# An attention and state-space kernel on one core: overdue SSM steps get a turn on VectorE, SSM units wait for their buffers before a bank, PV takes any ready tile, and 18 slots

## The chip, the cores and the metric

The kernel runs on one core of a Trainium2 chip. The metric is the device time of one execution, in microseconds (us). Engines are named as the profile names them: PE is TensorE (matmuls), PEld its weight loads, DVE is VectorE, ACT is ScalarE, POOL is GpSimd, SP is SyncE. "Span" is the time from the first to the last instruction of the profiled execution, some 1.7 us less than the time of that execution.

## The reference

Two independent halves are computed from their own inputs and joined along the last axis, to 1 x 2048 x 1280 in bf16. Cut to what matters:

```python
def ssm(x, ...):                      # 2048 steps, 640 states, complex
    Bu = einsum("bld,pd->blp", x, B_bar)
    for t in range(L):
        h = Lam_bar * h + Bu[t]       # diagonal: a scan for each state
    return 2 * einsum(h, C).real + x * Dskip

def attention(x, wq, wk, wv, wo):     # 32 query heads of 20, one key/value head
    scores = einsum("bhqd,bkd->bhqk", q, k) * 20 ** -0.5
    return einsum("bhqk,bkd->bhqd", softmax(scores), v) @ wo
```

The attention has 32 x 2048 x 2048 scores, and each wants an exponential. That is the large piece of work. The kernel cuts it into 2048 tiles of 128 keys x 512 query rows: 32 blocks of 64 tiles.

## The kernel before

A Python program orders the instructions when the kernel is built. It keeps a list of operations, each with an engine, an estimated duration, dependences and a priority (lower goes first), plays them against a clock of its own, and writes one fixed stream for each engine with semaphores between them. So a change of a priority changes no arithmetic; it changes the order of the streams, and which engine a tile falls to. The choice on each engine:

```python
    def pick(self, eng):
        ...                                   # `can`: all operations that could start now
        for op in can:
            p, dur = op.prio, op.dur
            if eng == "pe" and op.mode != self.mode:
                dur += self.SWITCH
                if p > self.URGENT:
                    p += self.STAY
            if urgent is not None and p > self.URGENT and t + dur > urgent + self.slack.get(eng, 1e9):
                continue
            if best is None or (p, op.seq) < key:
                best, key = op, (p, op.seq)
        return best
```

The exponential of a tile is taken on one of two engines. ScalarE empties score banks in turns of three and of two tiles (`PR<-SC`, 1536 and 1024 columns; with scores held in banks called SC). VectorE takes single tiles, called D tiles here: one eviction (`DR<-MB`) writes an integer whose bits are roughly the exponential, and three scaled copies of it (`DR<-DR`, for one tile or for two at once) correct the shape of the curve; four matmuls then use them. A D tile is taken when a side bank (MB) and four buffers ("slots") are free:

```python
    NDS = 16                                  # slots
    SHARE = 0.25

    def want_d(self, taken=0):
        s = self.s
        if self.tile_n >= NTILE - 8 or self.d_count + taken + 1 > self.SHARE * (self.tile_n - 16):
            return False
        if len(self.d_banks()) <= taken:
            return False
        return len(self.d_free()) > taken + len(self.SHIFTS) - 1
```

The share of tiles on VectorE is thus no constant; it falls out of how soon VectorE frees banks and slots. The product with the values (PV) keeps a queue for each of the four row groups, and looks at the head of each queue:

```python
        for j in range(4):                    # in pv_source
            if q[j]:
                e = q[j][0]
                if e[4].end is not None and s.seen(e[4], "pe") <= t and self.vp_seen(e[1], t):
                    group.append((j, e))
```

The state-space half (SSM) runs beside the attention as background: 40 half units (a projection on TensorE in one of two side banks, then on VectorE products, a scan and products again) and 20 output pieces ("y pieces"), dated evenly over the tiles. The side banks also carry the D tiles. On VectorE the SSM steps have priority 3, against 0.5 for the D tiles' steps, so they run when there is nothing else to do. `unit_ready` asks only for the data of a unit, and a unit can take a bank while the buffer into which its product goes is still in use:

```python
    def gate_of(self, key):
        o = self.buf_user.get(key)
        return lambda: o is None or o.start is not None

    SSM_FROM, SSM_TO = 110, 1830
        ...                                   # in background
        step = (self.SSM_TO - self.SSM_FROM) / len(jobs)
        ...
            T.append((self.SSM_FROM + step * i, 2) + job)

    def unit_ready(self, tb, c, ri):
        if ri == 1:
            return (tb, c, 0) in self.p_op
        ...                                   # tables, inputs, the unit before
```

## Time and profile before

| | before |
|---|---|
| median of the runs | 796.67 us (796.21 to 798.23, 4 runs) |
| profiled run, its span | 796.33 us, 794.6 us |
| mean granted clock | 1.000 |
| ScalarE busy / VectorE busy / TensorE busy | 772.1 / 730.9 / 732.6 us |
| tiles on ScalarE / on VectorE | 1668 / 380 |

From the page of before: busy time of each engine, VectorE's busy share in tenths for 40 equal slices of the span, the chain of work that ended last, and the costliest groups (out<-in, count, busy us and mean ns of one, idle time of the engine just before them and what ended most of it).

```profile
PE 732.6 (92%) x10441; PEld 240.5 (30%) x10441; DVE 730.9 (92%) x1818; ACT 772.1 (97%) x692; POOL 13.5 (2%) x35
...
DVE  6999999999999989999999999898999996789794
...
ACT 82%; PE 10%; DVE 5%; DMA 1%; issue 1%; ACTq 0%; DVEq 0%
...
L1007 ACT ACTIVATE PR<-SC 128x1536 bf16<-128x1536 f32 (+1 forms) x667 | 755.3, 1452 | 5.2 <-PE SC L538 3.2
...
L553 DVE TENSOR_SCALAR DR<-MB 128x512 int16<-128x512 f32 x380 | 254.2, 682 | 25.2 <-PE MB L538 23.3
...
L553 DVE TENSOR_SCALAR DR<-DR 128x512 int16<-128x512 int16 (+1 forms) x890 | 241.5, 320 | 6.6 <-PE MB L538 3.3
```

ScalarE is busy for 97% of the span and its exponentials are 82% of the chain. The other two engines show 92%, but they are not the bound: TensorE waits 37.8 us for ScalarE's banks (by the page, before its score matmuls) and VectorE 23.3 us for scores. VectorE's row of tenths is the second thing to see. It has room in it near the end (6, 7, 8, 9, 7, 9), where the steps of the SSM units are over (the last one on VectorE starts at 654.7 us).

The same groups by form, and a stretch of ScalarE's timeline (start, length, instructions; in brackets the idle time before and what ended it):

```profile
L1007 ACT ACTIVATE PR<-SC 128x1536 bf16<-128x1536 f32 x334 | 555.5, 1663 | 3.9 <-PE SC L538 2.9 <-PE MB L538 0.9
L1007 ACT ACTIVATE PR<-SC 128x1024 bf16<-128x1024 f32 x333 | 413.2, 1241 | 1.3 <-PE MB L538 0.8 <-PE SC L538 0.3
```

```profile
25.06 5.97 ACT L1007 ACTIVATE PR<-SC 128x1536 bf16<-128x1536 f32 x5 [2.08 <-PE SC L538]
...
105.09 95.03 ACT L1007 ACTIVATE PR<-SC 128x1024 bf16<-128x1024 f32 x84
...
754.52 28.89 ACT L1007 ACTIVATE PR<-SC 128x1536 bf16<-128x1536 f32 x25
```

The sum of the two forms, 968.7 us, is longer than the span, because neighbouring exponentials overlap. The pitch is the honest cost: 84 of them, 42 of each form, in 95.03 us are 2.262 us for five tiles, 0.4525 us a tile. The Trainium skill, "ScalarE: Activation LUTs", section "What ACT_TABLE_LOAD costs", gives 0.833 ns for an element of a row and an overlap of about 93 ns between neighbours. The trace agrees on the first, (1663 - 1241) / 512 = 0.82 ns; the overlap is longer by these records, 1663 + 1241 - 2262 = 642 ns for two, so 321 ns each.

25.06 us pass until the first exponential (the head), and 11.2 us from the end of the last one, 783.41, to the end (the tail).

ScalarE's waits (line waiting, what for, us in total, times, longest), and a table of stretches (stretch, length, then busy us and count of PE, PEld, DVE, ACT and POOL, granted clock, DMA share, GB/s):

```profile
ACT PR L1007 <- PE SC L538: 3.2, 4, 2.1
...
ACT PR L1007 <- PE MB L538: 1.7, 4, 0.8
```

```profile
784.55 0.69 DVE L1197 CAST pvsb<-MB 128x512 bf16<-128x512 f32 x1 [3.37 <-PE MB L538]
```

```profile
660.00:700.00 40.00, 38.09 (x628) 12.95 (x628) 29.86 (x79) 39.98 (x36) 0.00 (x0) 1.00 0.10 29
700.00:740.00 40.00, 35.86 (x485) 11.49 (x482) 35.36 (x90) 40.00 (x36) 0.00 (x0) 1.00 0.05 12
740.00:760.00 20.00, 17.89 (x224) 5.54 (x221) 16.55 (x40) 20.00 (x19) 0.00 (x0) 1.00 0.03 9
```

Line 1007 is the exponentials. ScalarE has next to no gaps to close. Outside the head and the tail, a gain has to come from giving it fewer tiles, and the last table says where VectorE has room: 18 us in these 100 us.

### The profile page before, as it was taken

How to read it: one execution, taken by the hardware profiler on the slowest of the kernel's cores; microseconds unless marked ns; L12 is line 12 of the kernel's file. 1: busy time of each engine (PE TensorE's matmuls, PEld its weight loads, DVE VectorE, ACT ScalarE, POOL GpSimd, SP SyncE). 2: the span in 40 equal slices, each digit the busy share in tenths (PEclk: the TensorE clock that was granted, in tenths of full speed). 3: DMA queues.
4: the chain of work that ended last, by engine and by line, in shares of the span. 5: the costliest groups of instructions: out<-in, count | busy, mean ns of one | idle time of the engine just before them, and what ended most of it. 6: DMA issues, size and time to landing. Idle time of an engine off the chain costs nothing.

```text
span 794.6 us, 24290 instructions
## 1 busy us (share of the span) xinstructions
PE 732.6 (92%) x10441; PEld 240.5 (30%) x10441; DVE 730.9 (92%) x1818; ACT 772.1 (97%) x692; POOL 13.5 (2%) x35
## 2 busy tenths in 40 slices
PE   7988888989889999999989999999999999998888
PEld 3322222222233322333223322232222323232224
DVE  6999999999999989999999999898999996789794
ACT  6899999999999999999999999999999999999995
POOL 6000000000000000000000000000000000000000
PEclk9999999999999999999999999999999999999999
DMA  9740200000000000020000000100000001000001
GB/s 210 118 86 9 50 10 9 7 4 9 9 9 23 16 21 23 16 49 16 10 8 23 23 23 22 36 16 15 9 15 9 23 22 30 29 15 9 7 11 36
DMA packets 54187, 21.60 MB, mean 27 GB/s; under 512 B 43464, under 2 KB 54080, under 8 KB 54080
## 3 DMA queue, kind: packets, MB, share of 16 engines
q1 hardware_dynamic: 52072, 19.87, 11.0%
q8 instruction: 82, 1.34, 0.7%
q10 hardware_dynamic: 2008, 0.18, 0.2%
q14 instruction: 25, 0.20, 0.1%
HBM read 7.20 MB, written 5.50 MB: 16 GB/s over the span
## 4 chain that ended last, share of the span: by engine, by line
ACT 82%; PE 10%; DVE 5%; DMA 1%; issue 1%; ACTq 0%; DVEq 0%
ACT PR L1007 82%; PE MB L538 4%; PE SC L538 3%; DVE DR L553 3%; PE MB L534 3%; PE SC L534 1%; DMA vrow<-in_A_Dskip_dram 1%; DVE prod L548 0%; DVE WO L683 0%; DVE xbT L760 0%; DMA dn<-sums 0%; DVE pvsb L1197 0%; DMA sums<-pvsb 0%; ACTq L519 0%; DVE fr L553 0%
## 5 line engine op out<-in xcount | busy, mean ns | idle before, releaser
L1007 ACT ACTIVATE PR<-SC 128x1536 bf16<-128x1536 f32 (+1 forms) x667 | 755.3, 1452 | 5.2 <-PE SC L538 3.2
L538 PE MATMUL SC<-QT,KT 32*128 32x512 bf16 x1668 | 260.0, 384 | 49.3 <-ACT PR L1007 37.8
L553 DVE TENSOR_SCALAR DR<-MB 128x512 int16<-128x512 f32 x380 | 254.2, 682 | 25.2 <-PE MB L538 23.3
L538 PE MATMUL MB<-PR,VP 128*32 128x512 bf16 x1668 | 253.5, 385 | 1.5 <-DVE pvsb L1197 1.3
L538 PE MATMUL MB<-DR,VS 128*32 128x512 bf16 x1520 | 253.0, 385 | 0.6 <-DVE pvsb L1197 0.6
L553 DVE TENSOR_SCALAR DR<-DR 128x512 int16<-128x512 int16 (+1 forms) x890 | 241.5, 320 | 6.6 <-PE MB L538 3.3
L538 PEld LDWEIGHTS SC<-QT,KT 32*128 32x128 bf16 x1668 | 66.9, 91 | 304.9 <-ACT PR L1007 238.5
L538 PE MATMUL MB<-QT,KT 32*128 32x512 bf16 x380 | 140.4, 384 | 3.0 <-DVE DR L553 1.7
L538 PEld LDWEIGHTS MB<-PR,VP 128*32 128x32 bf16 x1668 | 61.5, 94 | 66.2 <-issue 52.1
L538 PEld LDWEIGHTS MB<-DR,VS 128*32 128x32 bf16 x1520 | 61.2, 94 | 55.8 <-issue 43.0
L534 PE MATMUL MB<-xaT,BT 128*32 128x512 bf16 x800 | 62.0, 382 | 0.0
L548 DVE TENSOR_TENSOR prod<-MB,Z 128x1024 bf16<-128x1024 f32 x40 | 48.6, 1215 | 3.9 <-PE MB L534 3.4
L538 PE MATMUL MB<-xbT,wqf 128*32 128x512 bf16 x640 | 48.6, 382 | 0.2 <-DVE DR L553 0.2
L538 PE MATMUL MB<-KT,VZ 128*32 128x256 bf16 x892 | 43.2, 274 | 0.0
L534 PE MATMUL MB<-WO,OT 128*32 128x128 bf16 (+1 forms) x928 | 42.4, 292 | 0.0
L538 PEld LDWEIGHTS MB<-QT,KT 32*128 32x128 bf16 x380 | 33.2, 91 | 22.4 <-issue 11.6
L1487 DVE TENSOR_TENSOR_SCAN g<-sc,hst,u 128x512 bf16<-128x512 f32 x30 | 37.9, 1272 | 0.0
L534 PE MATMUL MB<-CT,xbT 128*32 128x512 bf16 (+1 forms) x640 | 30.0, 301 | 0.3 <-issue 0.3
L534 PE MATMUL MB<-CT,W 128*32 128x512 bf16 (+1 forms) x640 | 30.2, 301 | 0.0
L1316 DVE CAST stg<-MB 128x512 bf16<-128x512 f32 x35 | 23.9, 683 | 4.1 <-PE MB L534 3.7
L548 DVE TENSOR_TENSOR prod<-g,tab 128x1024 bf16<-128x1024 bf16 x40 | 27.1, 678 | 0.1
L538 PEld LDWEIGHTS MB<-KT,VZ 128*32 128x32 bf16 x892 | 22.0, 96 | 12.6 <-issue 6.3
(122 smaller groups left out, 346.3 us busy)
## 6 DMA issues: line engine op xcount, KB each, us to landing
out_dram<-stg SPq DMA_DIRECT2D x35, 128.0 KB, 1.8
rdB<-recs SPq DMA_DIRECT2D x124, 32.0 KB, 1.8
CT<-in_B_x_dram SPq DMA_DIRECT2D x2, 640.0 KB, 5.4
WO<-in_B_wo_dram SPq DMA_DIRECT2D x4, 200.0 KB
wqf<-in_B_wq_dram SPq DMA_DIRECT2D x1, 680.0 KB, 5.5
out_dram<-PR SPq DMA_DIRECT2D x5, 128.0 KB, 2.0
sums<-pvsb SPq DMA_DIRECT2D x31, 4.0 KB
dn<-sums SPq DMA_DIRECT2D x31, 4.0 KB, 1.9
```

The lines of the kernel that those rows point to most:

```text
L534: r = e.matmul(out[32 * j:32 * j + 32], lhsT=lhsT[:, 32 * j:32 * j + 32], rhs=rhs, start=start, stop=stop, tile_position=(0, 32 * j), skip ...
L538: return lambda e: e.matmul(out, lhsT=lhsT, rhs=rhs, start=start, stop=stop, **kw)
L548: return lambda e: e.tensor_tensor(out, a, b, op)
L553: return lambda e: e.tensor_scalar(out, a, s1, s2, op0=op0, op1=op1)
L1007: ex = self.act(lambda e: e.activation(dst, t[:, 0:512 * n], ACT.Exp, scale=1.0 / UNIT), 0.8333 * 512 * n + 50, deps=[op], reads=[b.key fo ...
L1316: ev = self.dve(lambda e: e.tensor_copy(st, bank.ap), 620, deps=[prev], reads=[bank.key], writes=[key], prio=self.EV, gate=(lambda: last.e ...
L1487: o = self.dve(lambda e, ri=ri, init=init: e.tensor_tensor_scan(p.g[:, u, ri, :], rdec, p.u[:, ri, :], init, ALU.mult, ALU.add), 1280, dep ...
```

## The change

The intent is to fill that late room by moving SSM work later and more evenly, and so to let VectorE take more tiles. Five things change together:

- (A) An SSM step on VectorE that is overdue gets priority 0.4 and a little, ahead of the D tiles, at most once in 3.3 us after the last such step. The SSM priority is otherwise too low to finish on time when D tiles are always ready.
- (B) A unit takes a side bank only when the buffer that its first product needs is free, so that banks do not stand idle under a unit that cannot go on. The gates now ask for all users of a buffer.
- (C) PV takes any ready tile of each of the four queues; when slots are scarce it prefers those from VectorE, which free slots.
- (D) 18 slots in place of 16.
- (E) Other dates for the SSM work: from tile 90 to 1780 for the units, with the last five y pieces at 1780 and on, 20 tiles apart.

The core of the diff, with bookkeeping cut:

```diff
+    PAUSE = 3300.0
@@ begin
+        if op.late:
+            self.late_from = self.t + op.dur + self.PAUSE
@@ pick
             p, dur = op.prio, op.dur
+            if op.late and t >= self.late_from:
+                p = 0.4 + 0.02 * p
@@
-    NDS = 16
+    NDS = 18
+    SCARCE = 8
@@ pv_source
+        scarce = len(self.d_free()) < self.SCARCE
         for j in range(4):
-            if q[j]:
-                e = q[j][0]
-                if e[4].end is not None and s.seen(e[4], "pe") <= t and self.vp_seen(e[1], t):
-                    group.append((j, e))
+            can = [e for e in q[j] if e[4].end is not None and s.seen(e[4], "pe") <= t and self.vp_seen(e[1], t)]
+            if can:
+                group.append((j, next((e for e in can if e[6] == "VS"), can[0]) if scarce else can[0]))
@@ (tables: due at 30 * c + 10; units: due at their date + GRACE)
+        self.s.spawn(self.hurry(self.unit_due[tb, c] + self.GRACE, us + scans + carry + outs + ws))
+
+    def hurry(self, due, ops):
+        yield lambda: self.tile_n >= due or ops[-1].start is not None
+        for o in ops:
+            o.late = True
@@ gate_of
-        o = self.buf_user.get(key)
-        return lambda: o is None or o.start is not None
-    SSM_FROM, SSM_TO = 110, 1830
+        ops = self.buf_user.get(key, ())
+        return lambda: all(o.start is not None for o in ops)
+    SSM_FROM, SSM_TO, Y_STEP, GRACE = 90, 1780, 20, 40
@@ background
-        step = (self.SSM_TO - self.SSM_FROM) / len(jobs)
+        step = (self.SSM_TO - self.SSM_FROM) / (len(jobs) - NC)
-            T.append((self.SSM_FROM + step * i, 2) + job)
+            n = i - len(jobs) + NC
+            T.append((self.SSM_FROM + step * i if n < 0 else self.SSM_TO + self.Y_STEP * n, 2) + job)
@@ unit_ready
+        if not self.gate_of(f"prod{ri}")():
+            return False
```

More of the change, by code (lines that the diff above doesn't have):

```diff
@@ L24 @@
     __slots__ = ("eng", "fns", "dur", "deps", "prio", "reads", "writes", "prev", "gate", "hook", "start", "end",
-                 "seq", "land", "dma_key", "idx", "tail", "mode", "load")
+                 "seq", "land", "dma_key", "idx", "tail", "mode", "load", "late")
     def __init__(self, eng, fns, dur, deps=(), prio=5, reads=(), writes=(), prev=None, gate=None, hook=None,
@@ L33, in __init__ @@
         self.dma_key, self.land, self.tail = dma_key, land, tail
-        self.mode, self.load = mode, load
+        self.mode, self.load, self.late = mode, load, False
         self.start = self.end = None
@@ L61, in __init__ @@
         self.mode = None
+        self.late_from = 0.0
         self.loads = []
@@ L1183, in pv @@
             lhs, kc, rhs, key, _, h, vk = e
-            self.pvq[b][j].pop(0)
+            self.pvq[b][j] = [x for x in self.pvq[b][j] if x is not e]
             first = (b, j) not in self.pv_first
@@ L1426, in ssm_scalars @@
             tk, zk = f"tab{c}", f"Z{c}"
+            zs = []
             o = self.dve(self.ts(t0, sin, gim, None, ALU.mult), 250, deps=[tabs[c], sc_op] + ([o] if c else []), reads=[tk, "sc"],
                          writes=["prod3"], prio=3)
+            zs.append(o)
             o = self.dve(lambda e, c=c, cos=cos, gre=gre, t0=t0: e.scalar_tensor_tensor(
@@ L1431, in ssm_scalars @@
                 reads=[tk, "sc", "prod3"], writes=[zk], prio=3)
+            zs.append(o)
             o = self.dve(self.ts(t1, sin, gre, None, ALU.mult), 250, deps=[o], reads=[tk, "sc"], writes=["prod3"],
                          prio=3)
+            zs.append(o)
             o = self.dve(lambda e, c=c, cos=cos, gim=gim, t1=t1: e.scalar_tensor_tensor(
@@ L1436, in ssm_scalars @@
                 reads=[tk, "sc", "prod3"], writes=[zk], prio=3)
+            zs.append(o)
+            self.s.spawn(self.hurry(30 * c + 10, zs))
             self.z_op[c] = o
@@ L1481, in unit_rest @@
                                prio=3, reads=["prod0", "prod1"], writes=[f"u{ri}"], gate=self.gate_of("u")))
-        self.buf_user["prod0"] = self.buf_user["prod1"] = us[1]
+        self.buf_user["prod0"] = self.buf_user["prod1"] = us
         rdec = bass.AP(tensor=p.sc, offset=self.RDEC * NC + c, ap=[[28 * NC, 128], [0, 512]])
@@ L1491, in unit_rest @@
             scans.append(o)
-        self.buf_user["u"] = scans[1]
+        self.buf_user["u"] = scans
         gk = [f"g{u}_0", f"g{u}_1"]
+        carry = []
         if tb < NQB - 1:
@@ L1502, in unit_rest @@
             self.state_op[(tb, c)] = b
+            carry = [a, b]
         outs = []
@@ L1509, in unit_rest @@
             outs.append(o)
+        ws = []
         for ri, op in ((0, ALU.subtract), (1, ALU.add)):
@@ L1512, in unit_rest @@
                          prio=3, reads=["prod2", "prod3"], writes=[f"W{c}_{tb % 2}"], gate=lambda: tb != 1 or self.first_half_read())
-        self.buf_user["prod2"] = self.buf_user["prod3"] = w
-        self.buf_user[f"g{u}"] = outs[1]
+            ws.append(w)
+        self.buf_user["prod2"] = self.buf_user["prod3"] = ws
+        self.buf_user[f"g{u}"] = outs + carry
         self.w_op[(tb, c)] = w
+        self.s.spawn(self.hurry(self.unit_due[tb, c] + self.GRACE, us + scans + carry + outs + ws))
[3 more added lines that the diff above has]
+            o.late = True
     def w_of(self, tb, c, ri):
@@ L1557, in gate_of @@
     def gate_of(self, key):
-        o = self.buf_user.get(key)
-        return lambda: o is None or o.start is not None
-    SSM_FROM, SSM_TO = 110, 1830
+        ops = self.buf_user.get(key, ())
+        return lambda: all(o.start is not None for o in ops)
+    SSM_FROM, SSM_TO, Y_STEP, GRACE = 90, 1780, 20, 40
+    unit_due = {}
     def background(self):
@@ L1595, in background @@
                 job = (lambda tb=tb: self.y_ready(tb), lambda bank, tb=tb, c=c: self.y_task(tb, c, bank))
-            T.append((self.SSM_FROM + step * i, 2) + job)
+            n = i - len(jobs) + NC
+            if unit:
+                self.unit_due[tb, c] = self.SSM_FROM + step * i
+            T.append((self.SSM_FROM + step * i if n < 0 else self.SSM_TO + self.Y_STEP * n, 2) + job)
         T.sort(key=lambda t: t[0])
```

## The prediction

> **What bounds the kernel now.** ScalarE. By the page it is busy 772.1 of 794.6 us (97%), and the chain that ended last is 82% one line, the exp that empties the score banks. From its first exp at 25.1 us to the end of the last at about 783.4 us it idles only 4.9 us (the waits of ScalarE: 3.2 us for scores, 1.7 us for matmuls into side banks). The timeline has 84 exps back to back in 95.03 us: 2.262 us for one of 1536 and one of 1024 columns, 0.4525 us for each of its 1668 tiles. Outside stand a head of 25 us and a tail of 11 us. VectorE (730.9 us, 92%) takes 380 of the 2048 tiles (18.6%); a table by 20 us windows shows it 95 to 99% busy in most windows until 260 us, and at 13.5 to 18.4 of 20 us from 660 us on. That late time is wasted: the SSM work has ended by then.
>
> **What the change does.** No arithmetic is new; it moves instructions, and so VectorE's share of tiles. The order of the built instructions says:
> - ScalarE: 330 exps of 1536 columns instead of 334, 331 of 1024 instead of 333: 16 tiles leave it.
> - VectorE: 16 more score evictions; scaled copies go from 640 single and 250 double to 454 and 367 (18 slots leave two free together more often).
> - TensorE: 64 more PV matmuls on VectorE's tiles, 16 fewer on ScalarE's, 236 fewer 256-column fillers.
> - SSM work spreads to tile 1900 or so; tiles per 128 on VectorE are flatter (mostly 22 to 29, one dip to 14 at tiles 640 to 768, 34 at the end; before 20 to 31).
>
> **Cost.** ScalarE: the forms differ by 512 columns. The Trainium skill, "ScalarE: Activation LUTs", section "What ACT_TABLE_LOAD costs", gives 0.833 ns an element; the means here (1663 and 1241 ns, 0.82 ns) agree. So about 1.345 and 0.918 us a turn: 4 x 1.345 + 2 x 0.918 = 7.2 us less. VectorE, at the late timeline's pitch (eviction 0.62 us, single copy 0.23, double 0.335): +10 -43 +39, some +6 us, so about 737 of 788 us, 94%. TensorE gains about 6 us (64 x 0.385 / 4) and loses about as much filler.
>
> **How much is on the critical path.** All 7.2 us, as long as ScalarE stays fed. Given back: VectorE is fuller in tiles 128 to 640, where TensorE's in-order stream waits for it behind a side bank; I allow 1 us more ScalarE idle time. Head and tail keep nearly the same order, so within 0.5 us.
>
> **Predicted time: 790.0 us (-0.8%)**, 787.0 to 794.0 us 8 times in 10. Faster by over 2% (under 780.5): 1%. Within 2%: 98%. Slower by over 2%: 1%.
>
> **What would show it.** Exp busy time near 748 us (661 exps); ScalarE idle between first and last exp 4 to 8 us; VectorE near 94%, its windows after 660 us filled; fillers 656; tail about 11 us; exp pitch still 2.262 us a pair.
>
> **What would make it wrong.** If VectorE, fuller in tiles 128 to 640 and in the last 128, holds up TensorE's stream, waits of ScalarE for scores rise to 10 us or more and the gain is gone. If the SSM output pieces that now come up to the last tiles free side banks late, the tail grows. If the granted clock (1.00) falls with fewer fillers, matmuls lengthen, though ScalarE hides most of it.

## The result, and the profile after

Ratios in this document are the mean time of one kernel's runs over the mean of the other's runs of the same rounds, so they are not quite the ratio of the medians quoted. Executions over 1.5% slower than the fastest of the same kernel are left out of the means. The bracket after a ratio is its 95% interval.

| | before | after |
|---|---|---|
| median of the runs, us | 796.67 (796.21 to 798.23, 4 runs) | 787.52 (786.47 to 788.61, 4 runs) |
| ratio | | 0.9882 [0.9862, 0.9901] |
| profiled run / its span / its clock | 796.33 / 794.6 / 1.000 | 787.72 / 786.0 / 0.998 |
| head, until the first exponential | 25.06 | 25.41 |
| exponentials on ScalarE, busy | 755.3 | 747.4 |
| idle between them | 3.0 | 2.9 |
| tail, after the last | 11.2 | 10.3 |
| tiles on VectorE, exponential instructions on ScalarE | 380, 667 | 396, 661 |

The page of after, the lines that answer to those of before:

```profile
PE 727.8 (93%) x10253; PEld 237.8 (30%) x10253; DVE 736.9 (94%) x1765; ACT 764.3 (97%) x686; POOL 13.5 (2%) x35
...
DVE  5999999999999999999998999999899999988995
...
ACT 90%; PE 5%; DVE 3%; DMA 1%; issue 0%; ACTq 0%; DVEq 0%
...
L1015 ACT ACTIVATE PR<-SC 128x1024 bf16<-128x1024 f32 (+1 forms) x661 | 747.4, 1456 | 4.9 <-PE MB L546 2.6
...
L561 DVE TENSOR_SCALAR DR<-MB 128x512 int16<-128x512 f32 x396 | 262.7, 680 | 16.2 <-PE MB L546 14.1
L561 DVE TENSOR_SCALAR DR<-DR 128x512 int16<-128x512 int16 (+1 forms) x821 | 239.2, 342 | 2.9 <-PE MB L546 0.4
```

The groups are the same at other line numbers. VectorE has 16 more evictions (262.7 us for 254.2) and yet spends less on the copies (239.2 for 241.5), because more of them serve two tiles at once. By form:

```profile
L561 DVE TENSOR_SCALAR DR<-DR 128x1024 int16<-128x1024 int16 x367 | 137.0, 415 | 0.7 <-PE MB L546 0.2
L561 DVE TENSOR_SCALAR DR<-DR 128x512 int16<-128x512 int16 x454 | 110.1, 283 | 2.2 <-PE MB L546 0.2
```

Before had 250 and 640 of them. ScalarE's waits, its timeline at the two ends, and VectorE's first step of the tail:

```profile
ACT PR L1015 <- PE MB L546: 2.6, 3, 1.2
...
ACT PR L1015 <- PE SC L546: 2.1, 1, 2.1
```

```profile
25.41 5.97 ACT L1015 ACTIVATE PR<-SC 128x1536 bf16<-128x1536 f32 x5 [2.08 <-PE SC L546]
...
753.99 21.67 ACT L1015 ACTIVATE PR<-SC 128x1536 bf16<-128x1536 f32 x19
```

```profile
776.16 0.69 DVE L1207 CAST pvsb<-MB 128x512 bf16<-128x512 f32 x1 [3.27 <-PE MB L546]
```

The last exponential ends at 753.99 + 21.67 = 775.66, and the tail's first VectorE step starts 0.5 us after it. In before the same step came 1.14 us after (784.55 against 783.41). The table of stretches:

```profile
660.00:700.00 40.00, 37.47 (x628) 13.12 (x620) 37.70 (x92) 40.00 (x37) 0.00 (x0) 1.00 0.07 18
700.00:740.00 40.00, 37.63 (x539) 11.89 (x531) 35.42 (x93) 40.00 (x37) 0.00 (x0) 1.00 0.07 20
740.00:760.00 20.00, 17.71 (x228) 5.62 (x232) 19.97 (x47) 20.00 (x19) 0.00 (x0) 1.00 0.04 8
```

VectorE works 93.1 of these 100 us, where it was 81.8. But only 4 of the 16 moved tiles are here: the views of VectorE's groups from 660 to 760 us have 66 evictions, where before had 62. More than half of the 11.3 us is SSM work that came later: VectorE's busy time outside the D tiles is 14.5 us in this stretch, 8.1 in before. The moved tiles are where that SSM work had been. VectorE's evictions from 60 to 260 us, in before and then in after:

```profile
L553 DVE TENSOR_SCALAR DR<-MB 128x512 int16<-128x512 f32 x98 | 65.9, 680 | 2.0 <-PE MB L538 1.4
```

```profile
L561 DVE TENSOR_SCALAR DR<-MB 128x512 int16<-128x512 f32 x116 | 76.1, 677 | 0.7 <-PE MB L546 0.3
```

One thing is new and unwelcome, at 165 us:

```profile
160.00:165.00 5.00, 4.03 (x56) 1.24 (x48) 5.00 (x10) 5.00 (x6) 0.00 (x0) 1.00 0.50 108
165.00:170.00 5.00, 4.14 (x35) 0.90 (x33) 3.99 (x12) 4.31 (x4) 0.00 (x0) 0.68 0.35 62
170.00:175.00 5.00, 4.73 (x55) 1.50 (x51) 4.89 (x11) 4.47 (x4) 0.00 (x0) 0.98 0.01 4
```

The granted clock falls to a mean of 0.68 for 5 us, TensorE gets through 35 matmuls where it did 56, and ScalarE misses 0.69 + 0.53 = 1.22 us in the two stretches. The Trainium skill, "TensorE: Matmul & The Clock Gate", section "Part 1: The HAM clock gate (the "warmup" mystery)", tells of a gate with two states, half and full, set by activity in free-running windows of 3413 ns. The trace agrees: asked for a finer stretch, it gives a clock of 0.50 for the 3.40 us from 166.77 us on, and 1.00 before and after.

```profile
166.77:170.17 3.40, 3.40 (x30) 0.74 (x30) 2.39 (x8) 2.54 (x3) 0.00 (x0) 0.50 0.14 24
```

The page names an idle window as the cause, and in its section "A second HAM failure mode: psum-queue depth-cycling" many short idle times; here TensorE was busy 4.03 of the 5 us before the dip by the matmuls' records.

### The profile page after: what moved, and what is told of

It reads as the page before. It is cut to its first block, busy times and chain, and to the rows that moved or that the text cites. A ratio compares the mean times of both kernels' runs of the same rounds, so it can differ in the third digit from the quotient of the medians.

```text
span 786.0 us, 23805 instructions
## 1 busy us (share of the span) xinstructions
PE 727.8 (93%) x10253; PEld 237.8 (30%) x10253; DVE 736.9 (94%) x1765; ACT 764.3 (97%) x686; POOL 13.5 (2%) x35
## 4 chain that ended last, share of the span: by engine, by line
ACT 90%; PE 5%; DVE 3%; DMA 1%; issue 0%; ACTq 0%; DVEq 0%
ACT PR L1015 89%; PE SC L546 2%; PE MB L546 2%; DVE DR L561 1%; PE MB L542 1%; DMA vrow<-in_A_Dskip_dram 1%; PE SC L542 1%; DVE prod L556 0%; DVE WO L691 0%; DVE xbT L768 0%; DMA dn<-sums 0%; DMA sums<-pvsb 0%; ACTq L527 0%; DVE fr L561 0%; DVE g L1503 0%
## 5 line engine op out<-in xcount | busy, mean ns | idle before, releaser
L1015 ACT ACTIVATE PR<-SC 128x1024 bf16<-128x1024 f32 (+1 forms) x661 | 747.4, 1456 | 4.9 <-PE MB L546 2.6
L561 DVE TENSOR_SCALAR DR<-MB 128x512 int16<-128x512 f32 x396 | 262.7, 680 | 16.2 <-PE MB L546 14.1
L561 DVE TENSOR_SCALAR DR<-DR 128x512 int16<-128x512 int16 (+1 forms) x821 | 239.2, 342 | 2.9 <-PE MB L546 0.4
L546 PE MATMUL MB<-DR,VS 128*32 128x512 bf16 x1584 | 230.8, 384 | 0.2 <-DVE DR L561 0.2
L546 PE MATMUL MB<-PR,VP 128*32 128x512 bf16 x1652 | 226.6, 386 | 2.4 <-DVE pvsb L1207 1.8
L546 PE MATMUL MB<-QT,KT 32*128 32x512 bf16 x396 | 143.8, 384 | 2.0 <-DVE DR L561 1.0
L546 PEld LDWEIGHTS MB<-PR,VP 128*32 128x32 bf16 x1652 | 56.8, 94 | 69.7 <-issue 50.3
L546 PEld LDWEIGHTS MB<-DR,VS 128*32 128x32 bf16 x1584 | 56.6, 94 | 55.6 <-issue 33.8
L546 PE MATMUL MB<-KT,VZ 128*32 128x256 bf16 x656 | 33.8, 274 | 0.0
L1207 DVE CAST pvsb<-MB 128x512 bf16<-128x512 f32 x32 | 21.9, 683 | 5.2 <-PE MB L546 5.2
```

The source lines that it names most:

```text
L546: return lambda e: e.matmul(out, lhsT=lhsT, rhs=rhs, start=start, stop=stop, **kw)
L561: return lambda e: e.tensor_scalar(out, a, s1, s2, op0=op0, op1=op1)
L1015: ex = self.act(lambda e: e.activation(dst, t[:, 0:512 * n], ACT.Exp, scale=1.0 / UNIT), 0.8333 * 512 * n + 50, deps=[op], reads=[b.key fo ...
L1207: ev = self.dve(lambda e: e.tensor_copy(p.pvsb[:, slot, :], bank.ap), 620, deps=[op], reads=[bank.key], writes=[f"pvsb{slot}"], prio=self. ...
```

## The experiments

Twelve kernels ran, in three calls; those of one call ran on one chip beside the kernel before. All gave correct results. All edits are to the kernel after. Four theories and their rivals were put to the test:

1. The gain is the tiles that left ScalarE, 0.45 us each. Rival: it is shorter waits or a shorter tail.
2. Overdue priority (A) buys no tiles; it costs some, and pays by keeping SSM work out of the tail. Rival: it is what lets VectorE take more tiles.
3. The slots (D), bank rule (B) and PV rule (C) each buy tiles. Rival: they buy none, and only keep ScalarE fed. (The expectations of e5, e6 and e10 call this rival "theory 3".)
4. The dip of the clock near 165 us comes from one large zero fill on VectorE, which the schedule holds for shorter than it is: 2.19 us in the trace, 1.5 us in the schedule. Rival: it comes from elsewhere.

The accounting of each profiled run, in us. It is one execution of each kernel, not always a typical one: those of e6, e7, e9 and e10 were the slowest of their kernel's runs, those of e8 and e12 the fastest.

| run | tiles on VectorE | head | exponentials | idle between | tail | span | clock |
|---|---|---|---|---|---|---|---|
| before | 380 | 25.06 | 755.3 | 3.0 | 11.2 | 794.6 | 1.000 |
| after | 396 | 25.41 | 747.4 | 2.9 | 10.3 | 786.0 | 0.998 |
| e1_cap380 | 380 | 25.01 | 754.5 | 3.7 | 10.1 | 793.3 | 0.997 |
| e2_no_hurry | 404 | 25.12 | 744.1 | 4.0 | 23.7 | 796.9 | 0.998 |
| e3_no_pv | 390 | 25.11 | 750.7 | 3.5 | 11.2 | 790.5 | 1.000 |
| e4_only_pv | 402 | 25.17 | 745.4 | 8.5 | 23.8 | 802.8 | 0.989 |
| e6_no_bank | 393 | 25.47 | 749.7 | 10.1 | 10.3 | 795.6 | 0.994 |
| e7_wo_pool | 396 | 31.13 | 747.5 | 3.0 | 10.5 | 792.1 | 0.989 |
| e8_pool_mwn | 405 | 25.42 | 747.7 | 23.8 | 10.8 | 807.8 | 0.987 |
| e9_after_again | 396 | 25.51 | 747.7 | 4.7 | 10.3 | 788.2 | 0.993 |
| e10_no_slots_again | 397 | 25.77 | 747.6 | 8.3 | 10.8 | 792.4 | 0.996 |
| e11_best_a | 400 | 25.72 | 746.1 | 7.6 | 10.4 | 789.8 | 0.996 |
| e12_best_b | 401 | 25.37 | 745.2 | 2.7 | 10.6 | 783.8 | 1.000 |

### First call: the number of tiles, the overdue rule, the PV rule

The kernel before took 797.38 us on this chip (median of 11 runs, 795.95 to 800.93).

**e1_cap380** holds the tiles on VectorE at before's number and leaves all else as in after.

```diff
-        if self.tile_n >= NTILE - 8 or self.d_count + taken + 1 > self.SHARE * (self.tile_n - 16):
+        if self.tile_n >= NTILE - 8 or self.d_count + taken + 1 > min(380, self.SHARE * (self.tile_n - 16)):
```

> The changed kernel, with VectorE's tiles stopped at 380, the number of the kernel before; the order of instructions is unchanged up to the last block, where 16 tiles go to ScalarE instead. Theory 1 (nearly all of the gain is the 16 tiles that left ScalarE, 0.4525 us each): 787.5 + 7.2 = 794.7 us, exp busy time about 754.6 us in 667 exps, 0.997 of before. Rival A (the gain lies in the order: flatter load, PV order, fewer stalls, shorter tail): stays within 1.5 us of 787.5 us.

Measured: 795.5 us (793.95 to 796.82), ratio 0.9973 [0.9952, 0.9993]. The page of this kernel has

```profile
L1015 ACT ACTIVATE PR<-SC 128x1536 bf16<-128x1536 f32 (+1 forms) x667 | 754.5, 1458 | 5.8 <-PE MB L546 3.6
```

With the tiles taken away, most of the gain is gone: 0.9% of the 1.2%. Theory 1 holds, with a remainder of 0.3% that has another source, of which the shorter tail (10.1 against 11.2 us) is the visible part.

**e2_no_hurry** takes the overdue rule (A) away.

```diff
-            o.late = True
+            o.late = False
```

> The changed kernel without the overdue rule (no SSM step is ever marked late). The order of instructions then gives VectorE 404 tiles, 8 more than the change, but leaves two scans, four products, four W and all five output pieces of the last SSM quarter behind the last exp. Theory 1 alone (each tile off ScalarE is worth 0.4525 us): 787.5 - 3.6 = 783.9 us. Theory 2 (the rule buys no tiles, it costs some; what it buys is that no SSM work stands behind the last exp): exps about 3.6 us shorter, but the tail after the last exp grows from 10.3 to about 20 us, total about 794 us.

Measured: 798.95 us (797.32 to 800.73), ratio 1.0017 [0.9997, 1.0036], so the whole gain is gone. VectorE takes 404 tiles, eight more than with the rule, and ScalarE's exponentials are 3.3 us shorter, but the tail is 23.7 us, where some 20 were expected. ScalarE's and VectorE's timelines at the end:

```profile
794.04 0.60 ACT L1324 ACTIVATE PR<-SC 128x512 bf16<-128x512 f32 x1 [14.62 <-PE SC L542]
```

```profile
771.82 2.45 DVE L1503 TENSOR_TENSOR_SCAN g<-sc,hst,u 128x512 bf16<-128x512 f32 x2
...
782.36 0.69 DVE L1326 CAST stg<-SC 128x512 bf16<-128x512 f32 x1 [3.11 <-PE SC L542]
784.74 0.69 DVE L1326 CAST stg<-SC 128x512 bf16<-128x512 f32 x1 [1.69 <-PE SC L542]
```

The last unit's scan runs at 771.82, when the attention is nearly done, and five y pieces follow one another at 2.38 us each. Theory 2 holds: the rule costs tiles and pays in the tail. It costs 3.3 us of exponentials and saves 13.4 us of tail.

**e3_no_pv** lets PV look at the heads of its queues only; the preference for VectorE's tiles goes with it.

```diff
-            can = [e for e in q[j] if ...]
+            can = [e for e in q[j][:1] if ...]
```

> The changed kernel with PV taking only the head of each of the four queues, as before. Order of instructions: 390 tiles on VectorE (6 fewer than the change, 10 more than before), and more PV matmuls behind the last exp. Theory 1: 787.5 + 6 x 0.4525 = 790.2 us, plus about 0.65 us of tail (from the last exp's end to the start of the last PV eviction 1.15 us as before, 0.5 us in the changed kernel) = 790.9 us. If PV order matters by itself for feeding ScalarE, ScalarE's idle time between exps rises by more than 2 us.

Measured: 792.26 us (791.78 to 793.19), ratio 0.9934 [0.9914, 0.9954]; all six runs were at clock 1.000. It has 390 tiles, and the tail is as long as in before. The first step of the tail on VectorE:

```profile
780.48 0.69 DVE L1207 CAST pvsb<-MB 128x512 bf16<-128x512 f32 x1 [5.34 <-PE MB L546]
```

The last exponential ends at 779.34, so this is 1.14 us after it, as in before, and not 0.5 us as in after. In the built order 16 PV matmuls stand behind the last exponential in before and 4 in after: with any ready tile allowed, less is left over for the end. The PV rule is worth six tiles and 0.9 us of tail, 6 x 0.4525 + 0.9 = 3.6 us by this reckoning, which would be a ratio of (787.5 + 3.6) / 796.7 = 0.993, as measured. Two more differences are on the pages. TensorE is busy with PV matmuls for 246.4 us (on VectorE's tiles) and 250.4 us (on ScalarE's) here, and for 230.8 and 226.6 us in after although it has 18 more of them, so more of them run side by side. And VectorE waits 22.6 us for scores before its evictions here, 14.1 us in after.

**e4_only_pv** is the PV rule alone: 16 slots, no overdue rule, no bank rule, before's dates. (The gates still ask for all users of a buffer.)

```diff
-    NDS = 18
+    NDS = 16
-            o.late = True
+            o.late = False
-    SSM_FROM, SSM_TO, Y_STEP, GRACE = 90, 1780, 20, 40
+    SSM_FROM, SSM_TO, Y_STEP, GRACE = 110, 1830, 20, 40
-        step = (self.SSM_TO - self.SSM_FROM) / (len(jobs) - NC)
+        step = (self.SSM_TO - self.SSM_FROM) / len(jobs)
-            T.append((self.SSM_FROM + step * i if n < 0 else self.SSM_TO + self.Y_STEP * n, 2) + job)
+            T.append((self.SSM_FROM + step * i, 2) + job)
-        if not self.gate_of(f"prod{ri}")():
-            return False
```

> The kernel before with one part of the change: PV takes any ready tile of a head (with the preference for VectorE's tiles when slots are scarce); 16 slots, no overdue rule, the old plan and bank rule. Order of instructions: 402 tiles on VectorE, 22 more than before, but the five output pieces of the last SSM quarter stand behind the last exp. Theory 1 alone: 796.4 - 22 x 0.4525 = 786.4 us. Theory 2: exps 10 us shorter, tail about 22 us instead of 11.2, so 796 to 798 us, nothing gained in total.

Measured: 804.44 us (803.01 to 807.7), ratio 1.0090 [1.0067, 1.0113], at clocks of 0.985 to 0.994. It is the slowest of this call although it has 402 tiles on VectorE. I had the direction and not the size. The tail is 23.8 us, so the SSM work is late again, and the idle time between exponentials is 8.5 us. The PV rule alone keeps VectorE so well supplied with D tiles that the SSM steps, with their low priority, are pushed to the end: the parts of the change depend on one another. Taken with e2_no_hurry, which lacks only the overdue rule and has the same long tail, this says that the PV rule pays only beside the overdue rule. No run has these two alone.

### Second call: slots, bank rule, and the dip of the clock

The kernel before took 797.67 us here (median of 11 runs; ten from 796.36 up, and one of 3059.82).

**e5_no_slots** has 16 slots.

```diff
-    NDS = 18
+    NDS = 16
```

> The changed kernel with 16 copy slots instead of 18. Order of instructions: 397 tiles on VectorE (one more than the change), but 511 single and 340 double copies instead of 454 and 367, about 4.7 us more VectorE time at 0.23 and 0.335 us. Theory 1 (only the number of tiles that left ScalarE counts): 787.5 - 0.45 = 787.1 us. Theory 3 (the slots buy pairs, and without them VectorE, already 94% busy, starves ScalarE): ScalarE's idle time between first and last exp rises from 2.9 us by more than 2 us, total above 789.5 us.

Measured: 793.37 us (median of all six; the five fast ones 791.09 to 795.86), ratio 0.9941 [0.9918, 0.9964]. The profiled run was the odd one, 1465.77 us, so its trace was not used. It has 397 tiles on VectorE by its built order: the two slots buy no tile.

**e6_no_bank** lets a unit take a bank as in before.

```diff
-        if not self.gate_of(f"prod{ri}")():
-            return False
```

> The changed kernel without the rule that an SSM unit takes a side bank only when its product buffer is free. Order of instructions: 393 tiles on VectorE (3 fewer), 521 single and 329 double copies. Theory 1: 787.5 + 3 x 0.4525 = 788.9 us. Theory 3 (a unit that holds one of the two side banks while it waits keeps score tiles out of it and stalls TensorE's stream): ScalarE idle time also up by more than 2 us, total above 790.5 us.

Measured: 795.07 us (793.96 to 797.44), ratio 0.9968 [0.9948, 0.9988]. It loses three tiles, which is 1.4 us, and the idle time between exponentials is 10.1 us in place of 2.9. Two stretches hold most of that:

```profile
60.00:80.00 20.00, 17.05 (x188) 4.91 (x180) 18.31 (x44) 17.18 (x16) 0.00 (x0) 0.91 0.03 8
...
100.00:120.00 20.00, 18.94 (x207) 5.08 (x207) 17.80 (x40) 15.95 (x15) 0.00 (x0) 0.83 0.03 9
```

ScalarE misses 2.82 and 4.05 us there, and the granted clock is 0.91 and 0.83. Whether the held bank makes the wait first and the clock falls after, or the other way round, these tables do not say. So the 10.1 us are not all the edit's: e9_after_again below, which has the bank rule, shows a dip at the same first place. At full clock this trace has three waits of 0.8 to 1.1 us (at 492, 526 and 632 us) that neither after nor e9_after_again has, and VectorE's waits for scores before its evictions are 21.4 us (14.1 and 15.2 there). That the loss belongs to the edit, and not to one execution, is in the six runs: none is below 793.96 us, and the two at a mean clock of 0.998 took 793.96 and 794.57 us, where the runs of after and of e9_after_again at that clock took 787.32 to 788.61.

**e7_wo_pool** moves the suspected zero fill from VectorE to GpSimd and leaves a fill of 16 elements (eight words) in its place, so that the order on the other engines stays word for word the same.

```diff
-        self.c_op["WO4"] = self.dve(lambda e: e.memset(p.WO4[:], 0.0), 1500, writes=["WO4"], prio=2.5,
-                                    gate=lambda: self.tile_n > 128)
+        wo = self.pool(lambda e: e.memset(p.WO4[:], 0.0), 3500, writes=["WO4"], prio=2.5, gate=lambda: self.started)
+        self.c_op["WO4"] = self.dve(lambda e: e.memset(p.WO4[0:1, 0, 0:16], 0.0), 1500, writes=["WO4"], prio=2.5,
+                                    deps=[wo], gate=lambda: self.tile_n > 128)
```

> The changed kernel with the one zero fill of the output weights (2.19 us on VectorE, plus 0.48 us of wait before it) moved to GpSimd, and a fill of eight words left in its place, so that the order on every other engine is word for word the same. Theory 4 (this fill, longer than the schedule thinks, is what starves TensorE around 158 to 170 us, where the granted clock falls to 0.68 in one 5 us window and ScalarE waits 1.2 us): clock 1.00 in all windows from 150 to 180 us, ScalarE idle between exps 1.2 us less, total 786.0 to 786.5 us. Rival (the dip has another cause, or the time is lost elsewhere): within 0.4 us of 787.5 us, clock still below 0.9 near 165 us.

Measured: 792.15 us (790.23 to 793.92), ratio 0.9928 [0.9908, 0.9948], so slower than after and not faster. The dip is still there, later by the longer head. The same place in this kernel, and then in e9_after_again, which is after unchanged and has the fill on VectorE:

```profile
170.00:175.00 5.00, 4.51 (x39) 1.02 (x39) 3.51 (x10) 3.97 (x5) 0.00 (x0) 0.66 0.01 2
```

```profile
165.00:170.00 5.00, 3.84 (x52) 1.20 (x48) 5.00 (x13) 5.00 (x6) 0.00 (x0) 1.00 0.57 105
```

Without the fill there is the dip, and with the fill, in another execution, there is none, so theory 4 falls. That execution has its dips elsewhere, near 65 and 240 us, so the place of a dip is not fixed by the order of the instructions. A transfer of the output weights runs just before the dip in after (DMA share 0.50 at 160 us), but e9_after_again has it too, so it does not decide either. The loss of e7_wo_pool is of my own making and sits in the head:

```profile
18.16 5.16 DVE L561 TENSOR_SCALAR fr<-iota,sc 128x512 int32<-128x512 f32 x1
...
18.67 4.36 POOL L691 MEMSET WO<- 128x5120 bf16 x1
```

A gate of the schedule fixes only the order at build time; it puts no wait into the stream. GpSimd reached the fill with nothing to wait for and ran it during the head, and the VectorE step beside it lasted 5.16 us (0.85 us in after). The first exponential then started at 31.13 and not at 25.41. The Trainium skill, "SBUF — State Buffer", section "SBUF: two separate sides", says that VectorE (in some of its modes) and GpSimd share a pair of ports, that the one that starts first has it for its whole instruction, and that the other is blocked. The end of the VectorE step, 23.32, just after the end of the fill, 23.03, agrees. VectorE's step began 0.5 us before the fill, but GpSimd was already at work on another step then (17.87 to 18.73 us), and the fill followed that one without a gap; so the order fits the page too. The records do not show the ports themselves.

**e8_pool_mwn** moves the zero fill (with its old gate) and 71 two-input steps to GpSimd (40 of the last step of the SSM units, 31 normalisations of the output), to free VectorE for more tiles.

```diff
-        self.c_op["WO4"] = self.dve(lambda e: e.memset(p.WO4[:], 0.0), 1500, writes=["WO4"], prio=2.5,
+        self.c_op["WO4"] = self.pool(lambda e: e.memset(p.WO4[:], 0.0), 3500, writes=["WO4"], prio=2.5,
-        self.norm_op[b] = self.dve(self.tt(p.OT[:, ot, :], ...), 350, deps=[o],
+        self.norm_op[b] = self.pool(self.tt(p.OT[:, ot, :], ...), 1300, deps=[o],
-            w = self.dve(self.tt(self.w_of(tb, c, ri), ...), 350, deps=outs,
+            w = self.pool(self.tt(self.w_of(tb, c, ri), ...), 1300, deps=outs,
```

> A try beyond the change: the zero fill, the 40 last additions of the SSM units (W) and the 31 normalising products go from VectorE (0.41 us each) to GpSimd, which is 2% busy; this gives VectorE 405 tiles, 9 more. If GpSimd does one in about 1.3 us and does not slow VectorE: 787.5 - 9 x 0.4525 = 783.4 us. If the two engines get in each other's way in SBUF, VectorE's copies lengthen from 0.23 and 0.335 us a turn, ScalarE idles more, and the total is at or above 787.5 us.

Measured: 811.77 us (809.62 to 816.4), ratio 1.0192 [1.0162, 1.0221], the slowest of all. VectorE does take 405 tiles, but ScalarE idles 23.8 us between exponentials. By form, from the views of GpSimd and of VectorE:

```profile
L556 POOL TENSOR_TENSOR OT<-pvsb,rdB 128x512 bf16<-128x512 bf16 x31 | 40.3, 1301 | 463.4 <-DMA rdB<-recs 453.4 <-PE MB L542 10.0
```

```profile
L561 DVE TENSOR_SCALAR DR<-DR 128x1024 int16<-128x1024 int16 x354 | 144.7, 451 | 0.5
L561 DVE TENSOR_SCALAR DR<-DR 128x512 int16<-128x512 int16 x507 | 141.6, 321 | 2.1
```

GpSimd needs 1301 ns for a normalisation that lasts 414 ns on VectorE in before (the SSM steps 1227 and 1238 ns), and VectorE's copies are 36 to 38 ns longer in the mean (415 and 283 ns in after). The mean hides what happens: by the trace, the 83 copies that overlap one of these 71 GpSimd steps last 751 and 669 ns in the mean, and the other 778 last 414 and 288 ns, about as in after. Over 861 copies that is 32 us of VectorE's time, against the 71 x 0.41 = 29 us that were taken off it. So nothing was freed. That the longer idle time of ScalarE comes of a schedule built for shorter copies is my reading of it, and no run tests it.

### Third call: after and 16 slots again, and two further versions

The kernel before took 797.72 us here (median of 11 runs, 796.25 to 801.75).

**e9_after_again** is the kernel after, unchanged, for a ratio on the same chip.

> The changed kernel itself, unaltered, beside the other three on one chip. If the first reading holds: 0.986 to 0.990 of before, runs at a mean granted clock of 1.000 near 786.5 us, and 1 to 1.5 us more for each 3 to 4 us stretch at half clock (a mean clock lower by about 0.002).

Measured: 789.64 us (787.68 to 790.05), ratio 0.9884 [0.986, 0.9908]. The ratio of the first measurement comes back, with absolute times 2 us higher and clocks of 0.993 to 0.998.

**e10_no_slots_again** repeats e5_no_slots.

> The changed kernel with 16 copy slots again, because the profiled run of e5 was an outlier (1465.77 us) and shows nothing of ScalarE's waits. Theory 3 (without pairs VectorE, at 94%, starves ScalarE): about 0.994 of before, ScalarE's idle time between first and last exp 2 us or more above the 2.9 us of the changed kernel, while exp busy time stays at 747 us. If the idle time is within 1 us of 2.9 us, theory 3 falls and the loss of e5 belongs to the chip's state.

Measured: 793.53 us (791.73 to 794.22), ratio 0.9932 [0.9908, 0.9956]. ScalarE's waits for side banks at the exponentials, in e9_after_again and then in e10_no_slots_again:

```profile
ACT PR L1015 <- PE MB L546: 4.1, 5, 1.5
```

```profile
ACT PR L1015 <- PE MB L546: 8.2, 9, 1.6
```

The number of tiles and the exponentials' busy time are the same (396 and 397 tiles, 747.7 and 747.6 us). The two slots buy 3.6 us of idle time: nine waits for TensorE become five. The clock is not the reason. Each of the two traces has two dips, and the waits in them and beside them are alike, 4.1 us of the 4.7 and 4.0 us of the 8.3; what is left is 0.6 us with 18 slots and 4.3 us with 16, most of it in three waits of 1.0 to 1.6 us at full clock (at 322, 393 and 723 us). The two slots also turn 57 single copies into 27 double ones (511 and 340 here; 454 and 367 with 18 slots). Two of the runs with 16 slots were at clock 1.000, and took 791.73 and 791.75 us, still slower than any run of e9_after_again. So on the slots the rival of theory 3 is right: they keep ScalarE fed.

**e11_best_a** and **e12_best_b** were chosen from many built variants by the schedule's own reckoning. Both split the zero fill in eight, have fewer staging buffers and more slots, and other priorities and dates.

```diff
e11_best_a
-        self.slack = {"pe": 60.0, "dve": 150.0}
+        self.slack = {"pe": 100, "dve": 200}
-    NDS = 18
+    NDS = 19
-    ALONE, TASK, PV = 1.9, 1.6, 2.0
+    ALONE, TASK, PV = 1.9, 1.7, 2.0
-    SSM_FROM, SSM_TO, Y_STEP, GRACE = 90, 1780, 20, 40
+    SSM_FROM, SSM_TO, Y_STEP, GRACE = 110, 1780, 16, 80
-    OVERDUE = 120
+    OVERDUE = 160
(staging buffers 4 to 3, fill in eight)
```

```diff
e12_best_b
-    PAUSE = 3300.0
+    PAUSE = 3000.0
-        self.slack = {"pe": 60.0, "dve": 150.0}
+        self.slack = {"pe": 30, "dve": 200}
-    NDS = 18
+    NDS = 20
-    KEEP = 3500.0
+    KEEP = 3900.0
-    ALONE, TASK, PV = 1.9, 1.6, 2.0
-    EV, P1, COPY, COPY1 = 0.52, 0.5, 0.49, 0.6
+    ALONE, TASK, PV = 1.5, 1.7, 2.0
+    EV, P1, COPY, COPY1 = 0.52, 0.5, 0.49, 0.55
-    SCARCE = 8
+    SCARCE = 7
-            self.s.spawn(self.hurry(30 * c + 10, zs))
+            self.s.spawn(self.hurry(20 * c + 10, zs))
-    SSM_FROM, SSM_TO, Y_STEP, GRACE = 90, 1780, 20, 40
+    SSM_FROM, SSM_TO, Y_STEP, GRACE = 110, 1740, 20, 10
-    OVERDUE = 120
+    OVERDUE = 160
(staging buffers 4 to 2, fill in eight)
```

> A version meant to beat both: the changed kernel with 19 copy slots (one staging buffer less), the zero fill of the output weights cut in eight, and other pacing (grace 80 tiles, SSM from tile 110, output pieces 16 tiles apart). Order of instructions: 400 tiles on VectorE, 4 more. Theory 1: 4 x 0.4525 = 1.8 us less than the changed kernel of the same call. If ScalarE's waits, at an even fuller VectorE, rise by as much, it is level.

> A second try: 20 copy slots (two staging buffers less), the fill cut in eight, SSM paced every 3.0 us, and the fillers called sooner (972 instead of 656). Order of instructions: 401 tiles on VectorE, 5 more. Theory 1: 2.3 us less than the changed kernel of the same call. If fillers hold the clock, the mean granted clock is 1.000 in all runs, worth about 1 us more against runs of the changed kernel at 0.998.

Measured: e11_best_a 791.27 us (787.22 to 792.31), ratio 0.9903 [0.9877, 0.9929]: no better than after, though it has four more tiles on VectorE. Its exponentials are 1.6 us shorter than e9_after_again's, and its waits between them are 2.9 us longer. e12_best_b 786.9 us (785.6 to 787.43), ratio 0.9855 [0.9829, 0.9881]: none of its runs is as slow as the fastest of e9_after_again (787.68), though the intervals of the ratios overlap. It is the fastest kernel here, by 0.3% by the ratios. Its waits at the exponentials, 2.1 us of which come before the first:

```profile
ACT PR L1016 <- PE MB L546: 2.7, 5, 0.9
ACT PR L1016 <- PE SC L546: 2.1, 1, 2.1
```

It has five tiles more than after (401), and it keeps the idle time at 2.7 us. It also has 972 of the filler matmuls that are there to keep TensorE's clock up, where after has 656, and its clocks are 0.996 to 1.000. That the fillers did it is not shown: more than a dozen other constants changed with them, and the number of fillers alone does not order the clocks (e6_no_bank has 864 and clocks of 0.994 to 0.998, e3_no_pv 800 and 1.000 in all six runs).

## Why the prediction was right

The prediction was 790.0 us, between 787.0 and 794.0, within 2%. The median is 787.52 us, 0.3% below, and inside the range. The mechanism was right; the points that held:

- **What bounds.** ScalarE, by the exponentials. After the change its share of the chain is 90%, and e1_cap380 shows that the time follows the tiles that leave it.
- **The exponentials.** Predicted 7.2 us less; measured 7.9 (755.3 to 747.4, and 661 of them as said). The pitch held: after has 393 of them back to back in 444.72 us, 2.263 us a pair. So the 16 tiles are 7.2 us. The other 0.7 us lies between before and e1_cap380, which have equally many tiles, and goes with the number of waits between exponentials in ScalarE's timeline: 7 in before, 3 in e1_cap380 and in after. A straight-line fit through the thirteen profiled runs gives 0.458 us of exponentials for each tile on ScalarE and 0.17 us for each such wait, and meets every run within 0.23 us (without e8_pool_mwn and its 29 waits: 0.458 and 0.14). A wait takes away an overlap of two neighbours, which would be the reason; no run tests that alone.
- **VectorE.** Predicted 737 us and 94%; measured 736.9 and 94%, with the late stretches filled as said (29.86 to 37.70 us of the 40 from 660 to 700 us, 16.55 to 19.97 of the 20 from 740 to 760). More than half of what filled them is SSM work, and most of the tiles came earlier, as the list of tiles per 128 had it.
- **TensorE.** 656 fillers, as said. Its busy time fell by 4.8 us (732.6 to 727.8), where the prediction had it about level. The clock, which was named as a risk, dipped once, to a mean of 0.68 over 5 us, and ScalarE missed 1.2 us there; that fewer fillers were the reason is not shown.

Besides the 0.7 us of the exponentials, two terms of the sum were mis-sized, and both fell on the fast side:

- **"I allow 1 us more ScalarE idle time."** It became 0.1 us less (3.0 to 2.9, where the prediction looked for 4 to 8), despite the dip. Here an execution counts too: e9_after_again, the same kernel with two dips, has 4.7 us. The step that failed was to take a fuller VectorE to mean more waits behind it. VectorE's own waits for scores fell too (23.3 to 14.1 us before the evictions); they are 22.6 us without the PV rule, 21.4 without the bank rule, and 18.0 without the two slots. e10_no_slots_again and e6_no_bank show what kept ScalarE's waits down: without the two slots the idle time is 8.3 us (4.7 with them on the same chip), without the bank rule 10.1 us (of which 6.9 lie in two stretches with dips). Both rules were in the diff, and I priced them for their tiles and copies only.
- **"Head and tail keep nearly the same order, so within 0.5 us."** The head rose 0.35 us, but the tail fell 0.9 us. e3_no_pv gives the cause: with the old PV rule the tail is 11.2 us again, and its first VectorE step comes 1.14 us after the last exponential and not 0.5 us.

One figure of the prediction was read wrongly: of the "4.9 us" of idle time from the first exponential on, 2.08 us lie before the first one. Between the first and the last there were 3.0 us, so no better order could win back more than that there. And "the SSM work has ended by then" holds for the units alone; y pieces went on until 703 us.

In sum, the parts by the profiled runs are -7.9 (exponentials), -0.1 (idle), -0.9 (tail), +0.35 (head), together -8.55 of the -8.6 us in the span.

The cause by part, as the experiments settle it: the PV rule buys six tiles and the shorter tail; the bank rule buys three tiles and fewer waits (how much of its 10.1 us of idle time is the edit's, and how much the dips', is open); the slots buy fewer waits of ScalarE and cheaper copies; and the overdue rule costs eight tiles and is what keeps 13 us of SSM work out of the tail, without which all the rest is lost (e2_no_hurry, e4_only_pv). These do not add up to 16, and should not: e4_only_pv has 402 tiles on the PV rule alone. Left open: the new dates (E) and the preference for VectorE's tiles when slots are scarce were not tried alone; the cause of the clock's dips was not found, after theory 4 fell; and one odd execution each of before and of e5_no_slots, on one chip, has no explanation.

## What to carry to other kernels

When the bounding engine is 97% busy without gaps, count the work that leaves it and price it by the pitch of a back-to-back stretch; then treat each scheduling rule of a change as two things, the work that it moves and the waits that it makes or takes away, and price both. A rule that lets the urgent work always go first needs a second one that stops the background work from piling up at the end: the PV rule, worth some 4 us here (ratio 0.9934 without it, 0.9882 with it), lost 7 us alone. And when schedules built for an estimated time are compared, those with the most work moved are not the fastest; run the candidates, and compare them on one chip at the same granted clock.

## What the Trainium skill lacked or had wrong

- "TensorE: Matmul & The Clock Gate" names an idle window ("Part 1: The HAM clock gate (the "warmup" mystery)") and frequent short idle times ("A second HAM failure mode: psum-queue depth-cycling") as causes of the half clock, with no figure for how busy is busy enough. Here the clock fell to a mean of 0.68 over 5 us after 5 us in which TensorE was 4.03 us busy by the matmuls' records. That these can be modelled ends, not activity of the array, may be the reason; no run settles it. An unchanged kernel dipped at 167 us in one execution and at 64 and 238 us in another.
- No page prices such a dip for a kernel that another engine bounds. In before's runs on one chip the mean clock went with the time: 795.95 to 796.93 us at 1.000, 797.33 to 797.48 at 0.998, 798.92 to 799.10 at 0.996, 800.27 to 800.93 at 0.994. That is 1 to 1.6 us for each 0.002; in the one dip of after ScalarE missed 1.2 us. On the other two chips the slowest runs have the lowest clocks too, but runs at 1.000 and at 0.998 overlap (796.25 to 798.24 and 796.97 to 797.75 us on the last one).
- "GPSIMD Engine Reference", in its opening paragraphs, says that VectorE is roughly 2 times faster at elementwise work; its measurement, in section "3.1 Elementwise — side-by-side cycle accounting", is of fp32 tiles with 2048 elements a row. A product of two 128x512 bf16 operands took 1301 ns on GpSimd and 414 ns on VectorE, 3.1 times. VectorE's copies that overlapped such a step lasted 669 ns for 288 (one tile) and 751 for 414 (two).
- "ScalarE: Activation LUTs", section "What ACT_TABLE_LOAD costs", gives 93 ns for the overlap of neighbouring instructions. By the records here it is 321 ns (1663 + 1241 ns for a pair with a pitch of 2262 ns). The page's own durations are some 200 ns shorter, so that its pitch for such a pair, worked out as an estimate from it, is 2.32 us, within 3% of the measured one.
- No page tells of rare executions that last far longer: on one chip one of before took 3059.82 us and one of e5_no_slots 1465.77 us, both at a recorded mean clock of 1.000.
